# Recurrent outputs of three batches computed with tokens on the partitions, rows shifted by DMA, and loads and weight conversion placed earlier

## The chip, the cores and the metric

One core of a Trainium2 chip runs the whole kernel. The metric is the device time in microseconds (us) of that core, and the numbers compared are medians over runs. Profiles show one execution; its times count from the start of its span. Engines are called as in the profile: PE (TensorE, its weight loads PEld), DVE (VectorE), ACT (ScalarE), POOL (GpSimd), SP (the queue that issues every DMA here).

## What is computed

An mLSTM cell runs over 4 batches, 8 heads, 768 tokens and head size 40. Its output, laid side by side over the heads (320 features), goes through a Fourier mixing step and an MLP of width 1280. Everything is float32.

```python
for t in range(S):                                   # mLSTM, per batch and head
    m_new = max(f[t] + m, i[t])
    C = exp(f[t] + m - m_new) * C + exp(i[t] - m_new) * outer(v[t], k[t])
    n = exp(f[t] + m - m_new) * n + exp(i[t] - m_new) * k[t]
    y[t] = sigmoid(o[t]) * (C @ q[t]) / max(|n . q[t]|, 1)
...
u  = x + real(fft(fft(x, axis=1), axis=2))           # x: y, heads side by side
un = (u - mean(u)) / sqrt(var(u) + 1e-6)
out = u + relu(un @ w_ch1) @ w_ch2
```

## The kernel before

**Chunks and halves.** The recurrence is computed in 6 chunks of 128 tokens. In batch 0 a chunk is one block; in batches 1 to 3 (the second to the fourth; the code counts from 0) it is two halves of 64 tokens, so that TensorE works as four tiles of 64 rows by 64 columns and a product of one half and one head occupies one tile. For one such chunk (`plan_halves`, L726) the steps are: load q and k with features on partitions (`qk`), v and k with tokens on partitions (`kvt`), running maxima (`W<-M_d`), decays (`Gb<-G_d`) and the output gate (`so`); turn maxima into weights with 8 Exp on ACT (L464), mask them on POOL (L487), form the scores on PE (`halves_scores`, L603), multiply them into W on DVE (`halves_weigh`, L640); add this chunk's part to the state (`halves_to_state`, L614; decay on POOL L629, add on DVE L636/L638). The numerators and denominators come from two sets of products into PSUM tile `ph`: `halves_from_state` (L645, stationary a 40x64 block of the state, moving 64 scaled queries) and `halves_from_chunk` (L657, stationary 64x41 values, moving 64x64 weights W). It comes in two parts; between them ACT reads one element (`halves_between`, L668, shown as `warm`), so that the second part waits until the first has been written. All these products go through one helper line, L491, so rows of L491 are told apart by their tiles. A float32 product is two PE instructions.

**The turn.** `ph` then has features on partitions and tokens along the row. ACT copies it to SBUF (`mlstm_heads`, L559 to L579: one copy of 512, and for some chunks one or two copies of a single token; chunks named in `BACKWARDS` are copied in reverse), PE transposes it in four 128x128 steps (`halves_turn`, L677, shown at L681), and DVE divides, applies the gate and writes `x` (`mlstm_finish`, L684 to L703). The products and the transposes' result lie in one PSUM tile `heads` of two banks; `side(0)` and `side(1)` are its halves. The Fourier step pairs token t with token 768-t, hence the reversed chunks; token 0 of chunks 0, 1 and 2 changes place, by `h_first` and small copies.

**Order.** Nothing is scheduled by a tool: `at(slot, phase, fn)` writes work into a table, and it is emitted sorted by slot and phase (EVAC 0, FILL 1, MAIN 2, FILL_PE 3 within a slot), each engine and SP taking its own in that order. The MLP of one batch is spread over 32 slots (`MLP_SLOTS`) and the mLSTM of the next batch is laid between its products, 3 slots per chunk. Batch b's mLSTM begins in slot 0, 32, 50 and 82, its Fourier step in 22, 54, 83 and 115, its MLP in 31, 63, 95 and 127. Pairs of chunks are folded on DVE (`mix_fold`, L770) 18, 21 and 22 slots after the mLSTM began, the last one slot later in batches 2 and 3.

**Weights and early loads.** w_ch1 and w_ch2 arrive as ten pieces of float64 that are unpacked by integer work (`Piece`, L355): `take` is two DVE instructions, `convert` two on ACT, `join` three on DVE; the list `when` (L1308) gives each piece's slots, and from the sixth on a piece is loaded one slot after the join of the piece two before it. `gates` (L141) computes running maxima M and decays g for all batches, and `maxima_out` (L304) and `halves_of_chunks` (L307) write them to DRAM as M_d and G_d, from which each chunk loads.

The functions that the change touches, with what calls them:

Of the kernel before, what the change touches and what calls it, by code (L numbers as in the profile page):

```python
# [19 lines left out]
L = 128  # L20
# [20 lines left out]
BACKWARDS = (2, 4, 5)  # L41
PAIRS = ((0, 5), (1, 4), (2, 3))
ORDER = (0, 5, 1, 4, 2, 3)
M_INIT = -1.0e30
# [8 lines left out]
def kernel(  # L53
# [87 lines left out]
    def gates(gp):  # L141
# [44 lines left out]
        for t in hT_bufs + Cd_bufs:  # L186
            nc.gpsimd.memset(t, 0.0)
# [115 lines left out]

        def maxima_out():  # L304
            nc.sync.dma_start(out=M_d.rearrange("c i p t -> p c i t"), in_=M[0:BH].rearrange("p c (i t) -> p c i t", i=2))

        def halves_of_chunks(step):  # L307
# [8 lines left out]
            elif step == 1:  # L316
# [3 lines left out]
                nc.sync.dma_start(out=G_d[:, H:].rearrange("c p t -> p c t"), in_=g[H:BH])  # L320
# [12 lines left out]
            else:  # L333
                pt, pd = late["p2"]
                nc.vector.tensor_copy(out=colT[:, :, 1, H:], in_=pt[:, :, H:])
                nc.vector.tensor_copy(out=decB[:, NP:], in_=pd[:, NP:])

        at(12, FILL + 0.7, maxima_out)
        at(1, FILL + 0.2, parts, last)
# [9 lines left out]
        for n, (s, phase) in enumerate(((16, FILL + 0.2), (18, FILL + 0.3), (19, FILL + 0.4), (21, FILL_PE + 0.5),  # L349
                                        (26, FILL + 0.8))):  # L350
            at(s, phase, halves_of_chunks, n)
# [90 lines left out]
    def mlstm_queries(b, c):  # L442
        return slice(LH if b > 0 and c == 0 else 0, L)
# [40 lines left out]
    def mlstm_mask(b, c):  # L484
        for i in range(2):
            W = chunks[b, c].W[i * LH:(i + 1) * LH]
            nc.gpsimd.affine_select(out=W, in_=W, compare_op=OP.is_ge, fill=0.0, base=0, pattern=[[0, H], [1, LH]],  # L487
                                    channel_multiplier=-1)
# [70 lines left out]
    def mlstm_heads(b, c, ph, parts=False):  # L559

        k = chunks[b, c]
        hT, before = k.hT, hT_bufs[(b * NT + c - 1) % 2]
        if b > 0:
            hT, before = (t.rearrange("p (hip m) t -> p hip m t", hip=2) for t in (hT, before))
        every, first, later = (tuple([slice(None)] * (len(ph.shape) - 1) + [t]) for t in
                               (slice(0, L), slice(0, 1), slice(1, L)))
        if c in BACKWARDS:
            nc.scalar.copy(out=hT[later], in_=backwards(ph, L - 1, L - 1))
            if c > TG:
                nc.scalar.copy(out=hT[first], in_=ph[first])  # L570
            else:
                nc.gpsimd.tensor_copy(out=k.hT[:, :, 0:1], in_=h_first)
        else:
            for r in (slice(hip * 64, hip * 64 + D1) for hip in range(2)) if parts else (slice(0, L),):
                nc.scalar.copy(out=hT[r], in_=ph[r])
            if c == 0:
                nc.gpsimd.tensor_copy(out=h_first, in_=k.hT[:, :, 0:1])
        if 0 < c < TG:
            nc.scalar.copy(out=before[first], in_=ph[first])  # L579
# [14 lines left out]
    def side(n):  # L594
        return banks["heads"].rearrange("p hip (s m t) -> p s hip m t", s=2, t=L)[:, n]

    TILES = ((0, 0), (1, 1), (0, 1), (1, 0))

    def columns(c, n):

        return LH if c == 0 else n

    def halves_scores(b, c):  # L603
# [5 lines left out]
        for p in range(NP):  # L609
            for hip, i in TILES:  # L610
                r, t = slice(hip * 64, hip * 64 + D), slice(i * LH, (i + 1) * LH)
                product(k.ps[t, hip, p, :], k.qk[r, 1, p, t], k.qk[r, 0, p, t], True)

    def halves_to_state(b, c):  # L614
        k = chunks[b, c]
        for p in range(NP):
            for i, hip in TILES:
                if 2 * c + i < NS - 1:
                    r, h, n = slice(i * LH, (i + 1) * LH), hip * NP + p, columns(c, D)
                    product(k.pc[hip * 64:hip * 64 + n, i, p, :], k.k[r, h * D:h * D + n], k.vw[r, h, :], True)  # L620
# [11 lines left out]
    def halves_add(b, c, i):  # L632

        k, n = chunks[b, c], 2 * c + i
        if n == 0:
            nc.vector.tensor_copy(out=halves_state(k, 1), in_=k.pc[:, 0])  # L636
        elif n < NS - 1:
            nc.vector.tensor_tensor(out=halves_state(k, i + 1), in0=halves_state(k, i + 1), in1=k.pc[:, i], op=OP.add)  # L638
# [6 lines left out]
    def halves_from_state(b, c):  # L645

        k = chunks[b, c]
        k.ph = side(0)
        for m in range(2):
            for i in range(2):  # L650
                for hip, e in TILES:
                    if 2 * c + i > 0:
                        r, t, p = slice(hip * 64, hip * 64 + D), slice(i * LH, (i + 1) * LH), 2 * m + e
                        product(k.ph[e * 64:(e + 1) * 64, hip, m, t], k.C[i][r, p * D1:p * D1 + LH], k.qg[r, p, t],
                                m == 0 and i == (c == 0))

    def halves_from_chunk(b, c, turn):  # L657
# [4 lines left out]
        for m in range(2):  # L662
            for i, e in TILES:
                hip, n = i ^ turn, columns(c, D1)
                r, h = slice(i * LH, (i + 1) * LH), hip * NP + 2 * m + e
                product(k.ph[e * 64:e * 64 + n, hip, m, r], k.v[r, h * D1:h * D1 + n], k.W[r, h, :], False)

    def halves_between(b, c):  # L668

        nc.scalar.copy(out=warm[0:1, 0:1], in_=chunks[b, c].ph[0:1, 1, 1, L - 1:L])  # L670

    def halves_gather(b, c):
        k = chunks[b, c]
        k.hT = hT_bufs[(b * NT + c) % 2]
        mlstm_heads(b, c, k.ph)

    def halves_turn(b, c):  # L677
        k = chunks[b, c]
        px = side(0 if c == NT - 1 else 1)
        for p in range(NP):  # L680
            nc.tensor.transpose(px[:, p // 2, p % 2], k.hT[:, p, :], ident)  # L681
        k.px = px

    def mlstm_finish(b, c):  # L684

        k = chunks.pop((b, c))
        if c == 0:
            xs[b] = x_bufs[b % 2]
        px = k.px.rearrange("p (a pr) t -> p a pr t", a=2) if b == 0 else k.px
        h1 = px.rearrange("p a pr (two e) -> p a (pr two) e", two=2)  # L690
# [11 lines left out]
        x, sc = (t.rearrange("p (a h d) -> p a h d", a=2, d=D) for t in (xs[b][:, c, 0:DM], k.so))  # L702
        nc.vector.tensor_tensor(out=x, in0=h1[:, :, :, 0:D], in1=sc, op=OP.mult)  # L703

# [21 lines left out]
    def plan_halves(b, s0, stride=3):  # L726
        for c in range(NT):
            s = s0 + stride * c
            end = c == NT - 1
# [4 lines left out]
            at(s, FILL, mlstm_load_o, b, c)  # L734
# [10 lines left out]
            at(s + 1, MAIN + 0.7, halves_weigh, b, c)  # L745
            at(s + 3, MAIN - 0.1 if end else FILL_PE, halves_from_state, b, c)
            at(s + 3, MAIN - 0.1 if end else FILL_PE, halves_from_chunk, b, c, 0)
            at(s + 3, MAIN if end else FILL_PE + 0.5, halves_between, b, c)
            at(s + 3, FILL_PE + 3, halves_from_chunk, b, c, 1)
            at(s + 4, FILL - 0.6, halves_gather, b, c)  # L750
            at(s + 4, FILL + 0.35, mlstm_tanh, b, c)
            t = s0 + (7, 10, 13, 16, 19, 19)[c]
            at(t, FILL_PE + 0.5, halves_turn, b, c)
            at(t + 1, MAIN + 0.55, mlstm_finish, b, c)
# [519 lines left out]
    def plan_batch(b, s_mlstm, s_mix, s_mlp):  # L1274
# [9 lines left out]
        else:  # L1284
            feat = [s_mix + c for c in ((3, 4, 6) if b == 1 else (3, 4, 7))]
            add = [s_mix + c for c in ((4, 4, 5, 6, 7, 7) if b == 1 else (4, 4, 5, 6, 8, 9))]
# [13 lines left out]
    plan_batch(2, 50, 83, s_mlp + 2 * MLP_SLOTS)  # L1300
    plan_batch(3, 82, 115, s_mlp + 3 * MLP_SLOTS)
# [144 lines left out]
```

## Time and profile before

| | before |
|---|---|
| median of 5 runs | 405.69 us (403.64 to 408.04) |
| profiled execution: time, span | 405.69 us, 404.0 us |
| granted TensorE clock | 0.999 |
| PE busy | 388.4 us (96%) |
| DVE busy | 280.5 us (69%) |
| ACT busy | 181.7 us (45%) |
| POOL busy | 131.7 us (33%) |
| DMA | 43.29 MB, mean 107 GB/s |

Busy time counts an instruction from its start to its end; PE's instructions overlap, so what PE really spends on a group is read from the distance between the starts of successive rows of its timeline. A row of the timeline is: start in us, length in us, engine, line, operation, written tile, tiles read, shape of the stationary operand, shape of the moving one, count. In the list of groups a row's last part is the idle time of that engine just before the group, with the instruction that ended it. In the list of waits the three numbers are total us, times, longest us. In the table by stretch the columns are the stretch, its length, then busy us (and instructions) of PE, PEld, DVE, ACT and POOL, granted clock, DMA share and GB/s.

### The profile page before, as it was taken

How to read it: one execution, taken by the hardware profiler on the slowest of the kernel's cores; microseconds unless marked ns; L12 is line 12 of the kernel's file. 1: busy time of each engine (PE TensorE's matmuls, PEld its weight loads, DVE VectorE, ACT ScalarE, POOL GpSimd, SP SyncE). 2: the span in 40 equal slices, each digit the busy share in tenths (PEclk: the TensorE clock that was granted, in tenths of full speed). 3: DMA queues.
4: the chain of work that ended last, by engine and by line, in shares of the span. 5: the costliest groups of instructions: out<-in, count | busy, mean ns of one | idle time of the engine just before them, and what ended most of it. 6: DMA issues, size and time to landing. Idle time of an engine off the chain costs nothing.

```text
span 404.0 us, 10669 instructions
## 1 busy us (share of the span) xinstructions
PE 388.4 (96%) x4246; PEld 284.0 (70%) x4246; DVE 280.5 (69%) x669; ACT 181.7 (45%) x510; POOL 131.7 (33%) x228
## 2 busy tenths in 40 slices
PE   8999999989899999998999999989999999999996
PEld 6877555556567677755569898856469997556996
DVE  7799977699858448676864679966764785336652
ACT  6887258587561232653472334644440023455000
POOL 5646414388862442241162424431220000020000
PEclk9999999999999999999999999999999999999999
DMA  7889498488554154365010635200000000000000
GB/s 224 292 234 305 108 237 255 118 268 239 156 182 132 60 138 133 92 186 147 0 44 2 176 108 156 86 4 2 0 2 16 18 35 32 0 2 0 32 34 32
DMA packets 23836, 43.29 MB, mean 107 GB/s; under 512 B 5076, under 2 KB 12972, under 8 KB 23660
## 3 DMA queue, kind: packets, MB, share of 16 engines
q1 hardware_dynamic: 23788, 42.63, 36.0%
q8 instruction: 33, 0.54, 0.6%
q14 instruction: 15, 0.12, 0.1%
HBM read 38.49 MB, written 4.12 MB: 105 GB/s over the span
## 4 chain that ended last, share of the span: by engine, by line
PE 78%; DVE 9%; DMA 4%; ACT 3%; issue 3%; POOL 1%; SPq 1%; POOLq 0%; ACTq 0%; DVEq 0%
PE po L1203 17%; PE pm L1084 17%; PE po L1147 8%; PE pm L1089 5%; PE pm L1022 5%; PE ph L491 4%; PE ps L491 3%; DMA qk<-in_qkT 3%; PE pu L901 3%; PE ph L681 2%; PE pz L870 2%; DMA raw<-in_w 1%; PE pm L1013 1%; PE put L944 1%; PE pz L858 1%
## 5 line engine op out<-in xcount | busy, mean ns | idle before, releaser
L1153 DVE SCALAR_TENSOR_TENSOR x<-po,rstd,x 128x160 f32<-128x160 f32 (+1 forms) x69 | 26.9, 394 | 38.0 <-PE po L1203 35.3
L1093 DVE TENSOR_TENSOR h<-h,pm 128x384 f32<-128x384 f32 x60 | 30.7, 550 | 31.1 <-PE pm L1084 17.2
L1084 PE MATMUL pm<-uT,w_sb 128*128 128x384 f32 x90 | 37.3, 501 | 0.2 <-DVE uT L1072 0.2
L464 ACT ACTIVATE W<-W,colT 128x64 f32<-128x64 f32 x144 | 37.4, 341 | 0.0
L1147 PE MATMUL po<-w_sb,h 128*128 128x320 f32 x120 | 34.4, 435 | 0.0
L487 POOL TENSOR_SCALAR_AFFINE_SELECT W<-W 64x512 f32<-64x512 f32 x36 | 29.1, 808 | 15.5 <-ACT W L464 14.3
L629 POOL TENSOR_TENSOR C<-C,decB 128x164 f32<-128x164 f32 x30 | 17.2, 573 | 50.3 <-DVE C L638 44.9
L1022 PE MATMUL pm<-uT,w_sb 128*128 128x384 f32 x80 | 29.6, 499 | 0.1
L1147 PEld LDWEIGHTS po<-w_sb,h 128*128 128x128 f32 x120 | 22.2, 190 | 9.4 <-issue 0.6
L474 POOL TENSOR_TENSOR qg<-qk,Gb 128x512 f32<-128x512 f32 (+1 forms) x21 | 28.2, 1341 | 0.9 <-DMA Gb<-G_d 0.8
L1203 PE MATMUL po<-T,S 128*128 128x160 f32 x180 | 28.0, 302 | 0.3 <-DVE x L1153 0.3
L1203 PEld LDWEIGHTS po<-T,S 128*128 128x128 f32 x180 | 25.5, 190 | 1.8 <-DVE x L1153 0.5
L1203 PE MATMUL po<-w_sb,h 128*128 128x160 f32 x180 | 26.4, 301 | 0.0
L1203 PEld LDWEIGHTS po<-w_sb,h 128*128 128x128 f32 x180 | 25.1, 190 | 1.2 <-DVE x L1153 0.3
L1089 PE MATMUL pm<-uT,w1t_sb 64*128 64x384 f32 x120 | 25.4, 510 | 0.0
L968 POOL TENSOR_TENSOR t<-rstd 128x6 f32<-128x6 f32 x12 | 3.1, 256 | 65.3 <-DVE v L962 64.8
L1084 PEld LDWEIGHTS pm<-uT,w_sb 128*128 128x128 f32 x90 | 15.5, 189 | 12.5 <-DVE h L1093 3.6
L1140 ACT ACTIVATE h<-h 128x384 f32<-128x384 f32 x45 | 23.1, 520 | 2.0 <-DVE h L1093 2.0
L670 ACT COPY warm<-ph 1x1 f32<-1x1 f32 x18 | 2.6, 147 | 45.9 <-PE ph L491 41.8
L480 POOL TENSOR_TENSOR vw<-kvt,colT 128x328 f32<-128x328 f32 x23 | 18.7, 813 | 13.9 <-DMA kvt<-in_kv 10.8
L949 ACT COPY uT<-put 128x384 f32<-128x384 f32 x24 | 11.1, 476 | 26.1 <-PE put L944 26.1
L937 ACT ACTIVATE uc<-x 128x384 f32<-128x384 f32 x24 | 14.6, 617 | 14.8 <-DVE x L929 14.8
(233 smaller groups left out, 879.4 us busy)
## 6 DMA issues: line engine op xcount, KB each, us to landing
kvt<-in_kv SPq DMA_DIRECT2D x24, 336.0 KB
qk<-in_qkT SPq DMA_DIRECT2D x48, 160.0 KB
raw<-in_w SPq DMA_DIRECT2D x10, 640.0 KB
Gb<-G_d SPq DMA_DIRECT2D x36, 128.0 KB
W<-M_d SPq DMA_DIRECT2D x36, 128.0 KB
so<-in_o SPq DMA_DIRECT2D x24, 160.0 KB
out<-x SPq DMA_DIRECT2D x24, 160.0 KB
ds_sb<-in_dft_s SPq DMA_DIRECT2D x1, 1155.0 KB
```

The source lines that it names most:

```text
L464: nc.scalar.activation(out=k.W[:, h, :], in_=M, func=AF.Exp, scale=-1.0, bias=colT[:, c, 0, b * H + h:b * H + h + 1])
L474: nc.gpsimd.tensor_tensor(out=k.qg[:, :, t], in0=k.qk[:, 0, :, t], in1=k.Gb[:, :, t], op=OP.mult)
L487: nc.gpsimd.affine_select(out=W, in_=W, compare_op=OP.is_ge, fill=0.0, base=0, pattern=[[0, H], [1, LH]], channel_multiplier=-1)
L491: nc.tensor.matmul(out, w, x, start=start, stop=True, skip_group_check=True)
L1022: nc.tensor.matmul(k.pm[i], w1_sb[:, ch, f0:f0 + L], u[2 * ch], start=(ch == 0 and not ahead), stop=(ch == 1 and ahead), skip_group_check= ...
L1084: nc.tensor.matmul(bank, w, u, start=start, stop=True, skip_group_check=True)
L1089: nc.tensor.matmul(bank, block(w1t_sb, i)[rows], mlp_u(gr, 1)[rows], start=False, stop=True, skip_group_check=True)
L1093: nc.vector.tensor_tensor(out=h, in0=h, in1=bank, op=OP.add)
L1140: nc.scalar.activation(out=h, in_=h, func=AF.Relu, scale=-1.0)
L1147: nc.tensor.matmul(k.po, hidden(gr, f)[:, i * L:(i + 1) * L], w2_sb[:, f, :], start=(f == 0), stop=(f == NFF - 1))
L1153: nc.vector.scalar_tensor_tensor(out=u, in0=po, scalar=k.rstd[:, c:c + 1], in1=u, op0=OP.mult, op1=OP.add)
L1203: nc.tensor.matmul(po, a[:, f], w[:, f], start=start and f == 0, stop=f == half - 1, skip_group_check=True)
```

## The change

In batches 1 to 3 the operands of the output products change places: the scaled queries and W become stationary (64 columns each) and the state and the values move (41 columns each), so `ph` has tokens on partitions. `halves_gather` and `halves_turn` go; `mlstm_finish` reads `ph` itself, one slot after the products. In chunks 0, 1 and 3 (the new `BACKWARDS`, for all batches) queries are laid out in reverse by the host, so their rows come out reversed; as a shift by one row is left over, their finish writes into `so` and `halves_rows` moves the rows into `x` by DMA, with two small POOL copies for chunk 2. For odd head pairs the two halves of keys and values are exchanged (in the host's layout, and on chip by `other_halves` and by an exchanged index in `maxima_out`), and the state's add reads PSUM with one more dimension. M and g are reversed for the backward chunks on POOL before they are written out. In the plan: batch 2 begins in slot 53 and batch 3 in 83; the output gate is loaded a slot sooner; tanh and finish come sooner; five pieces of w_ch2 are unpacked up to three slots sooner; one `mix_add` comes a slot later.

```diff
-BACKWARDS = (2, 4, 5)
+BACKWARDS = (0, 1, 3)
+RUNS = ((0, 2, True), (2, 3, False), (3, 4, True), (4, 6, False))
...
+        def other_halves():
+            odd = [colT[i * LH:(i + 1) * LH, :, 0, H + 1:BH:2] for i in range(2)]
+            kept = gp.tile([LH, NT, (BH - H) // 2], FP, name="kept")
+            for out, in_ in ((kept, odd[0]), (odd[0], odd[1]), (odd[1], kept)):
+                nc.gpsimd.tensor_copy(out=out, in_=in_)
         def maxima_out():
-            nc.sync.dma_start(out=M_d.rearrange("c i p t -> p c i t"), in_=M[0:BH].rearrange("p c (i t) -> p c i t", i=2))
+            m, in_ = (t.rearrange("p (n t) -> p n t", t=LH) for t in (free[0:BH, 0:S], flat(M, slice(0, NT))))
+            for c0, c1, back in RUNS:
+                n = slice(2 * c0, 2 * c1)
+                nc.gpsimd.tensor_copy(out=m[:, n], in_=backwards(in_[:, n], LH - 1, LH) if back else in_[:, n])
+            m = m.rearrange("p (c i) t -> p c i t", i=2)
+            for odd in range(2):
+                for i in range(2):
+                    nc.sync.dma_start(out=M_d[:, i ^ odd, odd:BH:2].rearrange("c p t -> p c t"), in_=m[odd:BH:2, :, i])
...
-                nc.sync.dma_start(out=G_d[:, H:].rearrange("c p t -> p c t"), in_=g[H:BH])
+                for c0, c1, back in RUNS:
+                    v = g[0:BH, c0:c1]
+                    if back:
+                        v = turned[:, at_:at_ + c1 - c0]
+                        at_ += c1 - c0
+                        nc.gpsimd.tensor_copy(out=v, in_=backwards(g[0:BH, c0:c1], L - 1, L))
+                    nc.sync.dma_start(out=G_d[c0:c1, H:].rearrange("c p t -> p c t"), in_=v[H:BH])
...
-                nc.vector.tensor_copy(out=colT[:, :, 1, H:], in_=pt[:, :, H:])
+                nc.vector.tensor_copy(out=colT[:, :, 1, H:BH:2], in_=pt[:, :, H:BH:2])
+                for i in range(2):
+                    nc.vector.tensor_copy(out=colT[i * LH:(i + 1) * LH, :, 1, H + 1:BH:2],
+                                          in_=pt[(1 - i) * LH:(2 - i) * LH, :, H + 1:BH:2])
...
+        at(13, FILL + 0.7, other_halves)
...
     def halves_from_state(b, c):
-        k.ph = side(0)
-        ...
-                        product(k.ph[e * 64:(e + 1) * 64, hip, m, t], k.C[i][r, p * D1:p * D1 + LH], k.qg[r, p, t], ...)
+        k.ph = banks["heads"][:, :, 0:NP * D1].rearrange("p hip (m d) -> p hip m d", d=D1)
+        ...
+                    product(k.ph[t, hip, p, :], k.qg[r, p, t], k.C[i][r, p * D1:(p + 1) * D1], p == 0)
     def halves_from_chunk(b, c, turn):
-                product(k.ph[e * 64:e * 64 + n, hip, m, r], k.v[r, h * D1:h * D1 + n], k.W[r, h, :], False)
+                product(k.ph[queries(c, i), hip, p, :], k.W[rows(j), h, :], k.v[rows(j), h * D1:(h + 1) * D1],
+                        2 * c + i == 0 and m == turn == 0)
-    def halves_gather(b, c):
-        ...
-    def halves_turn(b, c):
-        ...
     def mlstm_finish(b, c):
-        px = k.px.rearrange("p (a pr) t -> p a pr t", a=2) if b == 0 else k.px
-        h1 = px.rearrange("p a pr (two e) -> p a (pr two) e", two=2)
+        h1 = k.px.rearrange("p (a pr) (two e) -> p a (pr two) e", a=2, two=2) if b == 0 else k.ph
...
+        k.x = k.so if b > 0 and c in BACKWARDS else xs[b][:, c, 0:DM]
...
+    def halves_rows(b, c):
+        x, y = xs[b][:, :, 0:DM], chunks[b, c].x
+        def move(out, in_):
+            nc.sync.dma_start(out=out, in_=in_)
+        if c == 2:
+            nc.gpsimd.tensor_copy(out=x[0:1, 1], in_=x[0:1, 2])
+            nc.gpsimd.tensor_copy(out=x[0:1, 2], in_=x[0:1, 0])
+            move(x[0:1, 0], chunks[b, 1].x[L - 1:L])
+        elif c in BACKWARDS:
+            move(x[1:L, c], y[0:L - 1])
+            if c != 1:
+                move(x[0:1, c], y[L - 1:L])
...
-            at(s, FILL, mlstm_load_o, b, c)
+            at(s - 1, FILL, mlstm_load_o, b, c)
...
-            at(s + 1, MAIN + 0.7, halves_weigh, b, c)
-            at(s + 3, MAIN - 0.1 if end else FILL_PE, halves_from_state, b, c)
-            at(s + 3, MAIN - 0.1 if end else FILL_PE, halves_from_chunk, b, c, 0)
-            at(s + 3, MAIN if end else FILL_PE + 0.5, halves_between, b, c)
+            at(s + 1, FILL + 0.55 if b == 1 and c > 0 else MAIN + 0.7, halves_weigh, b, c)
+            at(s + 3, FILL_PE, halves_from_state, b, c)
+            at(s + 3, FILL_PE, halves_from_chunk, b, c, 0)
+            at(s + 3, FILL_PE + 0.5, halves_between, b, c)
             at(s + 3, FILL_PE + 3, halves_from_chunk, b, c, 1)
-            at(s + 4, FILL - 0.6, halves_gather, b, c)
-            at(s + 4, FILL + 0.35, mlstm_tanh, b, c)
-            t = s0 + (7, 10, 13, 16, 19, 19)[c]
-            at(t, FILL_PE + 0.5, halves_turn, b, c)
-            at(t + 1, MAIN + 0.55, mlstm_finish, b, c)
+            at(s + 3, FILL_PE + 0.6, mlstm_tanh, b, c)
+            at(s + (5 if (b, c) == (2, 2) else 4), FILL + 0.3 if b == 1 else MAIN + 0.55, mlstm_finish, b, c)
+            at(s + 6, FILL - 0.6, halves_rows, b, c)
...
-            add = [s_mix + c for c in ((4, 4, 5, 6, 7, 7) if b == 1 else (4, 4, 5, 6, 8, 9))]
+            add = [s_mix + c for c in ((4, 4, 5, 6, 7, 7) if b == 1 else (4, 5, 5, 6, 8, 9))]
...
-    plan_batch(2, 50, 83, s_mlp + 2 * MLP_SLOTS)
-    plan_batch(3, 82, 115, s_mlp + 3 * MLP_SLOTS)
+    plan_batch(2, 53, 83, s_mlp + 2 * MLP_SLOTS)
+    plan_batch(3, 83, 115, s_mlp + 3 * MLP_SLOTS)
...
-    when += [((33, 0.7), (35, 0.7), (36, 0.6))] + [((s, 0.7), (s + 1, 0.7), (s + 2, 0.6)) for s in (36, 39, 42, 45)]
+    when += [((33, 0.7), (34, 0.3), (34, 0.6)), ((34, 0.7), (35, 0.7), (36, 0.6))]
+    when += [((s, 0.7), (s + 1, 0.7), (s + 2, 0.6)) for s in (36, 39, 42)]
```

## The prediction, made before the change was run

> **What bounds the kernel now.** I read the page first: shares of the engines, then the chain that ended last, then the list of waits, then timelines and stretches.
>
> ```profile
> PE 388.4 (96%) x4246; PEld 284.0 (70%) x4246; DVE 280.5 (69%) x669; ACT 181.7 (45%) x510; POOL 131.7 (33%) x228
> ...
> PE 78%; DVE 9%; DMA 4%; ACT 3%; issue 3%; POOL 1%; SPq 1%; POOLq 0%; ACTq 0%; DVEq 0%
> ...
> L681 PE MATMUL ph<-ident,h 128*128 128x128 f32 x72 | 10.6, 276 | 0.0
> ```
>
> PE is busy nearly all the time and is 78% of the chain, so PE work that disappears should shorten the run, except in stretches where PE is only kept waiting. The 10.6 us of the turn are overlapping durations; what it really holds PE for is the distance between starts:
>
> ```profile
> 180.86 0.60 PE L681 MATMUL ph<-ident,h 128*128 128x128 f32 x4
> 181.30 0.81 PE L1084 MATMUL pm<-uT,w_sb 128*128 128x384 f32 x2
> ```
>
> Four transposes of a chunk cost 181.30 - 180.86 = 0.44 us. Next, where PE waits, and for whom:
>
> ```profile
> PE ph L491 <- DVE x L703: 3.9, 5, 1.3
> ...
> PE ph L491 <- ACT warm L670: 0.7, 1, 0.7
> PE ph L491 <- DVE W L643: 0.5, 1, 0.5
> ```
>
> The first is five waits of `halves_from_state` for the finish of an earlier chunk. The other two lie in one stretch that is not PE's:
>
> ```profile
> 75.00:105.00 30.00, 27.54 (x468) 16.43 (x469) 29.21 (x57) 22.18 (x63) 25.01 (x34) 1.00 0.77 218
> ```
>
> There DVE is busy 29.2 of 30 us and POOL 25.0: the mLSTM of batch 1 beside the unpacking of w_ch2. What PE saves there is not simply time saved.
>
> [...]
>
> ```profile
> 139.97 0.69 PE L491 MATMUL ph<-qg,C 40*64 40x64 f32 x32
> 140.49 0.41 PE L491 MATMUL ph<-W,kvt 64*41 64x64 f32 x16
> 140.71 0.65 PE L491 MATMUL ps<-qk 40*64 40x64 f32 x32
> 141.18 0.49 PE L491 MATMUL ps<-vw,kvt 64*40 64x41 f32 x32
> 141.49 0.41 PE L491 MATMUL ph<-W,kvt 64*41 64x64 f32 x16
> ...
> 116.22 0.63 PE L491 MATMUL ps<-vw,kvt 64*64 64x41 f32 x32
> 116.66 0.41 PE L491 MATMUL ph<-W,kvt 64*41 64x64 f32 x16
> ```
>
> By starts, 32 instructions cost 0.47 us with 64 stationary and 64 moving columns (140.71 to 141.18), 0.31 with 40 and 41 (141.18 to 141.49), but 0.44 with 64 and 41 (116.22 to 116.66). The last is the form of all new output products. So fewer moving columns bring next to nothing: the 64 stationary columns are the limit[...].
>
> **The change part by part.**
>
> *Turn.* 18 chunks x 0.44 = 7.9 us of PE go. Four of the 18 (86 to 111 us: L681 starts at 86.4, 94.8, 101.9, 110.6) lie in or next to the stretch where DVE and POOL set the pace; I count those 1.8 us as nothing. Gain 6.1, at most 7.9.
>
> *Output products.* From state 0.52 to about 0.47 to 0.50, from chunk 0.22 + 0.34 (the second to its successor at 141.83) to about the same plus 0.02, as the stationary side grows from 41 to 64 columns. I take 0; bounds from -1 us (gain) to +0.7 over 18 chunks.
>
> *Waits for the finish.* Now the finish of chunk c - 1 is planned in slot s + 1 and the next products into `ph` in slot s + 3, where s begins chunk c; before, the finish of chunk 3 stood in slot s0 + 17 and chunk 5's products in s0 + 18. Chunk 5's products of batches 2 and 3, 32 slots apart, started at 183.4 and 272.7 us in the timeline, so a slot is about 2.8 us, and the five DVE instructions of a finish are 0.16 + 0.17 + 0.20 + 0.64 + 0.49 = 1.66 us. Of 3.9 us I count 3.5.
>
> *ACT.* The copies of 18 chunks go (18 x 0.58 and a dozen of 0.17 to 0.18: about 12.6 us), but ACT is busy 45%; on the path they count only through L670, whose element read must run between two groups of products. For chunk 5 nothing of another kind now stands between the two groups, so PE waits there for the products' end, ACT's 0.15 us and two hand-overs: in the trace a chunk 5 showed 0.58 us of PEld waiting for it even with other products between. I charge 0.2 us x 3 = 0.6; bounds 0 to 1.5. Tanh (0.48) comes ahead of nothing PE needs.
>
> *DVE.* Finish is the same five instructions with another source. The state's add keeps its 164 elements (0.32). Weigh of batch 1 comes forward in its slot, ahead of the unpacking's long instructions. A piece is 0.64 + 0.68 + 0.95 + 1.25 + 1.09 = 4.6 us of DVE, 0.83 + 0.73 on ACT, and one 0.36 us issue on SP; five pieces move up to 3 slots ahead. From 65 to 75 us DVE was busy only 4.6 of 10 us, and can take one. The stretch held PE for 30 - 27.5 = 2.5 us; with a piece's DVE work out of it I count 1.0 regained, bounds -1 to 2.5. A join that waits for ACT now holds the adds behind it on DVE for at most ACT's 1.6 us.
>
> *POOL.* Chunk 2 gets two copies of 1x320. The nearest row, a copy of 1x161, took 0.66 us, so about 1.0 each; 2 us per batch, less the old `h_first` copies (0.41 each). For batches 2 and 3 POOL has room (7.3 us busy of 160 to 180). In batch 1 it doesn't: qg of chunk 4 ended at 106.8, its products started at 107.9. The copies sit ahead of that qg, so up to 1.5 us of PE wait; I charge 0.5. Before that they wait for DVE's finish and a landed row; masks and decays queue behind them.
>
> *Rows by DMA.* 6 issues per batch, 18 x about 0.35 us of SP. Row moves are issued at s + 6, the folds read them 3 slots later at least (chunk 3: s0 + 15, fold s0 + 18): 8 us of cover. [...] No run here shows such a move, nor SP's own price for it. Cost 0[...]. Loads behind them have 5 slots.
>
> *Early part.* M_d takes four issues instead of one and waits for four POOL copies, about 2 us (from a 32x384 row of 1.09 us); behind it on SP are the Fourier tables, issued at 32.5 and first used at 44.4. G_d takes four, behind two POOL copies: SP waited 8.3 us there for ACT until 44.7, now about 1.8 us more; behind it are batch 1's first loads, and SP next waited 1.5 us at 50.4 for a raw buffer, which absorbs most. `other_halves` is about 1 us of POOL. I charge 0.5; bounds 0 to 2.5, as the chain runs through a 6.6 us load at 54.8. The gate loaded a slot sooner (0.4 us of SP) needs one of four buffers that the row move must first release; it has a slot. The later starts of batches 2 and 3 (3 and 1 slots) leave their folds 7 and 9 slots ahead of the Fourier products; the `mix_add` a slot later stays ahead of its turn. Cost 0.
>
> **Sum:** 6.1 + 0 + 3.5 + 1.0 - 0.6 - 0.5 - 0.5 = 9.0 us. The profiled execution took 405.69 us (span 404.0), equal to the median: 405.7 - 9.0 = 396.7; I say 396.5.
>
> **Rivals.**
>
> *The columns count after all.* If 41 moving columns cost as 40/41 did (0.31 per 32), each chunk would save (0.52 + 0.56) - 0.62 = 0.46, times 18 = 8 us more: 388.5. Against it stands the 0.44 measured; even half of it gives 392. Chance 0.12.
>
> *New waits take the gain.* In 63 to 113 us DVE and POOL set the pace, and a faster PE merely waits; if the same holds in 225 to 260 us (DVE 28.4 of 35 us), another 1.5 us of turns and half of the 3.5 go, and the three costs reach their upper ends (5.5 for 1.6): 396.7 + 1.5 + 1.8 + 3.9, about 404. For it: 29.2 of 30. Against: from 120 us on PE shows almost no wait but those that go. Chance 0.17.
>
> *Row moves arrive late, slower than before.* SP takes its work in order and was held up to 5.9 us by a W load waiting for PE. A move stuck behind one comes 8 us later than planned, and a fold then stops DVE, with weigh and the MLP's adds behind it. It decides once a move lands more than 3 slots late: with 6 us in each of three batches, 18 us, against 9 gained, 415. Against it: the moves are emitted before the loads of their slot, and the page's W waits end with the slot. Chance 0.05.
>
> *The change doesn't do what it says:* products as before, no turn but the same stalls: 405.7 - 6.1 + 1.6, about 401. It is in the range.
>
> **Chances.** My forecast 0.66, columns 0.12, new waits 0.17, late rows 0.05. About 1% (4 us: 401.6 to 409.7) is what a measurement of this kernel can tell from no change. Faster by more: 0.66 + 0.12 + a quarter of the new waits = 0.82; within: 0.13; slower: 0.05. The range is 389 to 402: it takes in my bounds and most of the columns case.
>
> **What would show it.** No L681, PE's busy time down by 8 us or more; no wait for L703; blocks of 32 output products still 0.44 to 0.5 us apart; DVE busier at 65 to 75 us. Wrong would be: output products at 0.31, PE waiting for qg or W in 80 to 113 us by more than before, DVE's folds waiting for DMA, or the first MLP products later than before.

## The result, and the profile after

| | before | after |
|---|---|---|
| median | 407.11 us (403.57 to 410.51, 80 runs) | 408.72 us (406.85 to 411.00, 43 runs) |
| ratio to before, 95% interval | | 1.0049, 1.0033 to 1.0065 |
| profiled execution: time, span | 405.69, 404.0 us | 410.13, 408.4 us |

Half a per cent slower, where 396.5 us was forecast. The turn is gone, and yet nothing is gained. The page of the kernel after (busy time, the granted clock in 40 slices, the shares of the chain that ended last):

```profile
PE 385.9 (94%) x4174; PEld 280.4 (69%) x4174; DVE 278.7 (68%) x671; ACT 171.8 (42%) x481; POOL 133.0 (33%) x237
...
PEclk9999999899969999999999999999999999999999
...
PE 60%; DVE 22%; DMA 9%; issue 3%; ACT 2%; SPq 1%; POOL 1%; DVEq 0%; ACTq 0%; POOLq 0%
```

PE fell from 78% to 60% of the chain, DVE rose from 9% to 22%, DMA from 4% to 9%, and there are dips in the clock. PE's busy time fell by only 2.5 us, though transposes of 10.6 us went: a matmul on a slower clock is busy longer (those of L1053 start 0.64 us apart at half clock and 0.32 at full, below; with the row moves split, below, it is 380.5 us, 7.9 less than before). In PE's list of waits, the finish (now L720) is down from 3.9 to 0.4 us, as forecast; other rows take its place:

```profile
PE ph L519 <- ACT warm L699: 6.9, 8, 2.4
PE po L1234 <- DVE x L1184: 2.5, 3, 1.1
PE pm L1115 <- DVE h L1124: 1.3, 2, 1.0
...
PE ps L519 <- POOL vw L507: 1.2, 1, 1.2
...
PE ps L519 <- DMA qk<-in_qkT: 0.7, 2, 0.4
...
PE ph L519 <- DVE x L720: 0.4, 1, 0.4
```

**Where it is lost.** The first transpose of each batch's MLP (tile `put`) is an easy landmark. The stages between these landmarks, in us, from the starts of those rows in the timelines (this kernel and the experiments below). Each row is from one profiled execution. The two rows that begin batch 1's MLP, before and then after:

```profile
156.66 0.55 PE L944 MATMUL put<-ident,uc 128*128 128x128 f32 x3
```

```profile
163.53 0.55 PE L975 MATMUL put<-ident,uc 128*128 128x128 f32 x3
```

| kernel | to batch 0's `put` | to batch 1's | to batch 2's | to batch 3's | to the end |
|---|---|---|---|---|---|
| before | 56.0 | 100.7 | 83.4 | 84.3 | 79.6 |
| after | 55.8 | **107.7** | 83.6 | 80.5 | 80.8 |
| row moves of 112 + 15 | 54.7 | 99.7 | 83.6 | 80.5 | 80.9 |
| row moves of 126 + 1 | 55.2 | 99.4 | 83.5 | 80.5 | 80.9 |
| row moves of 113 + 14 | 55.8 | 101.9 | 83.6 | 80.5 | 81.0 |
| 112 + 15 in batch 1 alone | 54.9 | 99.6 | 83.7 | 80.5 | 81.1 |
| before, with nine moves of 127 | 55.4 | **104.3** | 83.4 | 84.3 | 79.7 |
| before, with nine of 112 + 15 | 55.8 | 99.4 | 83.4 | 84.7 | 79.8 |

The fourth stage gains 3.8 us of the 4.5 that its five turns (5 x 0.44 = 2.2) and its share of the finish's waits (2.3) promised. The third, with six turns, gains nothing; by its later start batch 2 has a chunk more to do there. The second, with batch 1's mLSTM in it, loses 7.0. Stretches of it (columns as in the table of stretches before), after, and then before:

```profile
60.00:130.00 70.00, 61.68 (x891) 36.59 (x890) 49.28 (x100) 35.79 (x106) 35.89 (x54) 0.93 0.62 171
...
111.00:117.00 6.00, 1.94 (x64) 1.50 (x64) 0.33 (x1) 3.44 (x13) 3.78 (x8) 0.92 0.25 72
117.00:123.00 6.00, 6.00 (x14) 3.19 (x10) 2.12 (x6) 0.59 (x2) 1.67 (x6) 0.52 0.70 171
```

```profile
60.00:130.00 70.00, 67.27 (x1112) 41.85 (x1112) 56.43 (x116) 42.29 (x127) 43.06 (x60) 1.00 0.67 195
```

In the 70 us, every engine and the DMA do less than before: no engine's share has risen, everybody waits. Between 111 and 117 us PE works 1.94 of 6 us and DVE 0.33; in the next 6 us PE is busy throughout, but on a clock of 0.52. In the trace PE runs at half clock from 116.0 to 122.8 us, 6.8 us, and the matmuls of L1053 start 0.64 us apart there instead of 0.32, which is 2.9 us on top of the wait. In the 3.4 us ahead (the length of the shorter of such stretches) PE worked 0.36 us, and its wait at 116 us was 2.4 us. In this case's profiles twelve more such stretches began between 70 and 240 us, each 3.4 or 6.8 us long; one is in this kernel, from 78.4 to 81.9 us, begun 1.7 us after a wait of 1.5 us for `warm` had ended. In the 3.4 us ahead of the twelve PE was busy for 1.4 to 2.2 us, and no wait there was longer than 2.7 us. So in these profiles waits of 1.2 to 2.7 us were followed by 3.4 or 6.8 us at half clock; what sets it off isn't shown. None of the changed kernel's executions had a mean clock above 0.995; of the 43 executions of the kernel before that ran beside the first experiments, 26 had 0.999 or more.

What they wait for stands in the chain of the kernel after (start, length, what):

```profile
98.27 2.92 SPq L454
...
101.66 11.09 DMA kvt<-in_kv
112.76 0.02 issue
112.77 0.03 SPq L728
...
112.83 0.65 SPq L728
113.48 0.05 issue
113.53 10.53 DMA x<-so
...
124.16 0.50 DVE eo L809
```

L728 is the issue of a row move, x<-so. The pair of moves issued around 113 us takes until 124, when DVE's fold can start; the load of keys and values issued 4 us after an earlier one takes 11.1. On SP's queue the same moves hold up the issues behind them (first the kernel after, then the one with rows split into 112 and 15):

```profile
97.55 0.68 SPq L728 DMA_DIRECT2D x<-so  x1
98.27 3.35 SPq L454 DMA_DIRECT2D qk<-in_qkT  x2
101.66 0.35 SPq L456 DMA_DIRECT2D kvt<-in_kv  x1
...
118.16 6.31 SPq L478 DMA_DIRECT2D Gb<-G_d  x2
```

```profile
111.57 1.28 SPq L478 DMA_DIRECT2D Gb<-G_d  x2
```

The 6.31 us are not spent in issuing. The two issues of `Gb` take 0.62 and 0.59 us in the trace, and between them SP waits 5.1 us for a row move to land. The loads don't need the moved rows, nor does L728 need the keys and values that it stands behind in the chain. In the trace SP's issues use eight completion semaphores (counters that tell that a transfer has landed) in turn: 240 issues, each semaphore 30 times, always eight issues apart, and an issue waits on the semaphore it uses, so until the transfer eight issues before it has landed. So a slow move also stops SP itself, eight issues later. SP's waits for row moves between 60 and 130 us, 16.6 us in all and none with the rows split:

```profile
SPq L478 <- DMA x<-so: 11.2, 2, 6.1
...
SPq L484 <- DMA x<-so: 5.4, 1, 5.4
```

**Theory A.** The 127 rows are the cause, by their number. In the trace this kernel's last move of 127 rows goes row by row, 127 packets mostly 52 ns apart and 55 ns each, and takes 6.8% of the 16 DMA engines, about one engine's share (the window is shown below). That the row count decides this was the author's assumption, not yet shown by a trace: 112 or 126 rows would be spread over several engines, and 113, a prime as 127 is, again over one. The experiments measure these counts. A move on one engine is slow itself, and by this theory every later load on 16 engines has a sixteenth of its rows on that engine, behind it. The packets of the load of keys and values issued at 101.66 us (128 packets of 2688 bytes, counted from the trace by start) look so:

| us | 102 to 103 | 103 to 104 | 104 to 105 | 105 to 106 | 106 to 111 | 111 to 113 |
|---|---|---|---|---|---|---|
| packets | 5 | 52 | 57 | 6 | 0 | 8 |

Eight is 128/16, one engine's share, though the trace doesn't name a packet's engine. The load is 120 rows done by 106 us, and the last eight come when a row move has passed. **Rival theories:** the new loads and moves are simply more DMA work; the earlier unpacking of weights crowds DVE; the finish and the element reads in their new slots make PE wait.

### The profile page after: what moved, and what is told of

Same layout as the page of the kernel before. It is cut to its first block, busy times and chain, and to the rows that moved or that the text cites. A ratio compares the mean times of both kernels' runs of the same rounds, so it can differ in the third digit from the quotient of the medians.

```text
span 408.4 us, 10572 instructions
## 1 busy us (share of the span) xinstructions
PE 385.9 (94%) x4174; PEld 280.4 (69%) x4174; DVE 278.7 (68%) x671; ACT 171.8 (42%) x481; POOL 133.0 (33%) x237
## 4 chain that ended last, share of the span: by engine, by line
PE 60%; DVE 22%; DMA 9%; issue 3%; ACT 2%; SPq 1%; POOL 1%; DVEq 0%; ACTq 0%; POOLq 0%
PE po L1234 17%; PE pm L1115 13%; PE po L1178 8%; DMA x<-so 5%; PE pm L1120 4%; DMA kvt<-in_kv 3%; PE pu L932 3%; PE ph L519 2%; PE ps L519 2%; DVE m L422 2%; DMA raw<-in_w 2%; DVE so L716 1%; DVE e L420 1%; PE pz L901 1%; PE pz L889 1%
## 5 line engine op out<-in xcount | busy, mean ns | idle before, releaser
L491 ACT ACTIVATE W<-W,colT 128x64 f32<-128x64 f32 x144 | 37.4, 338 | 9.7 <-DMA W<-M_d 9.7
L652 POOL TENSOR_TENSOR C<-C,decB 128x164 f32<-128x164 f32 x30 | 16.0, 534 | 75.4 <-DVE C L667 63.6
L1115 PE MATMUL pm<-uT,w_sb 128*128 128x384 f32 x90 | 37.6, 505 | 2.0 <-DVE h L1124 1.3
L1053 PE MATMUL pm<-uT,w_sb 128*128 128x384 f32 x80 | 32.9, 554 | 0.1
L515 POOL TENSOR_SCALAR_AFFINE_SELECT W<-W 64x512 f32<-64x512 f32 x36 | 27.3, 759 | 11.2 <-ACT W L491 9.6
L999 POOL TENSOR_TENSOR t<-rstd 128x6 f32<-128x6 f32 x12 | 3.3, 274 | 80.3 <-DVE v L993 79.7
L1115 PEld LDWEIGHTS pm<-uT,w_sb 128*128 128x128 f32 x90 | 15.6, 189 | 16.5 <-DVE h L1124 7.4
L1053 PEld LDWEIGHTS pm<-uT,w_sb 128*128 128x128 f32 x80 | 16.2, 216 | 11.8 <-issue 5.0
L1120 PE MATMUL pm<-uT,w1t_sb 64*128 64x384 f32 x120 | 23.4, 508 | 0.0
L519 PE MATMUL ph<-kvt,W 64*64 64x41 f32 x576 | 16.2, 231 | 7.0 <-ACT warm L699 6.9
```

The lines of the kernel that those rows point to most:

```text
L491: nc.scalar.activation(out=k.W[:, h, :], in_=M, func=AF.Exp, scale=-1.0, bias=colT[:, c, 0, b * H + h:b * H + h + 1])
L519: nc.tensor.matmul(out, w, x, start=start, stop=True, skip_group_check=True)
L1053: nc.tensor.matmul(k.pm[i], w1_sb[:, ch, f0:f0 + L], u[2 * ch], start=(ch == 0 and not ahead), stop=(ch == 1 and ahead), skip_group_check= ...
L1115: nc.tensor.matmul(bank, w, u, start=start, stop=True, skip_group_check=True)
L1120: nc.tensor.matmul(bank, block(w1t_sb, i)[rows], mlp_u(gr, 1)[rows], start=False, stop=True, skip_group_check=True)
```

## The experiments

Each ran beside the kernel before; ratios are to it, with 95% intervals, and a time is the median of that experiment's executions.

**Rows in two pieces, 112 and 15.**

```diff
-            move(x[1:L, c], y[0:L - 1])
+            move(x[1:113, c], y[0:112])
+            move(x[113:L, c], y[112:L - 1])
```

> Only edit to the changed kernel: each row move of 127 rows is issued as two, of 112 and of 15 rows. Theory A (a move of 127 rows runs on one DMA engine, holds it for about 10 us and delays every later load's share on that engine): the moves land within 3 us, the kernel takes about 397 us, ratio to before 0.97 to 0.985. Rival B (the new order of ACT and DVE work in batch 1, with the products' second part waiting for the element read, costs the time by itself): within 2 us of the changed kernel, ratio 1.00 to 1.01.

Measured: 401.10 us, ratio 0.9855 (0.9814 to 0.9897). The same bytes, with nine more issues on SP, and 7.6 us less than the changed kernel (7.9 by the two ratios). That is just outside theory A's 0.970 to 0.985 and far from rival B's 1.00. This one beats both kernels, and none of the later versions can be told from it as faster.

**No row moves.** Left out: rows of the reversed chunks 0, 1 and 3 stay one token off; their finish writes straight into `x`.

```diff
-        k.x = k.so if b > 0 and c in BACKWARDS else xs[b][:, c, 0:DM]
+        k.x = xs[b][:, c, 0:DM]
...
-            move(x[0:1, 0], chunks[b, 1].x[L - 1:L])
-        elif c in BACKWARDS:
-            move(x[1:L, c], y[0:L - 1])
-            if c != 1:
-                move(x[0:1, c], y[L - 1:L])
```

> The changed kernel without any row move by DMA: the rows of the reversed chunks stay unshifted, so this part of the computation is left out. It bounds what the moves cost in all. Theory A: no more than 2 us faster than the split moves, about 396 us, ratio 0.965 to 0.985. Rival B: as the changed kernel, 1.00 to 1.01.

Measured: 404.69 us, 0.9936 (0.9908 to 0.9965): neither theory's outcome, and the run tells less than it was meant to. Its profiled execution took 401.29 us at a clock of 1.000. Only three of the 22 executions had that clock (401.0 to 401.7 us); the other 19, at 0.982 to 0.996, took 403.6 to 409.1, and none of them has a profile, so what slowed them isn't shown. In the profile, the finish now writes `x` two slots sooner than the moves did, into a buffer that is still being stored: its L720 waited 2.0 us for a store, and PE behind it 2.4 us at 245.7 us, so the fourth stage is 82.4 us instead of 80.5. The second is the shortest of all, 97.5 us against 99.7 with split moves, whose profile has 3.4 us of half clock there; whether split moves still cost anything, this run can't tell.

**The moves alone, in the kernel before**, as nine transfers of 127 rows of 1 KB into a spare tile that nobody reads; then the same in 112 and 15 rows.

```diff
+    def spare_rows(b, c):
+        nc.sync.dma_start(out=rest[1:L], in_=done[b, c].so[0:L - 1, 0:2 * L])
...
+            if c in (0, 1, 3):
+                at(t + 3, FILL - 0.6, spare_rows, b, c)
```

> The kernel before, with nine moves of 127 rows of 1 KB (from the gate tile to an unused one) added two slots after the finish of chunks 0, 1 and 3 of batches 1 to 3. Theory A: slower than before by 3 to 9 us, ratio 1.007 to 1.022, with loads behind the moves landing up to 10 us late. Rival B: no change, 0.998 to 1.003.

> The kernel before with the same nine added moves as in the earlier run with 127 rows, cut into 112 and 15 rows. Theory A: the added bytes and issues cost nothing that shows, ratio to before 0.998 to 1.004. If the bytes, the SP issues or the wait for the gate tile were the cost, 1.006 to 1.010 as with 127 rows.

Measured: 410.29 us, 1.0081 (1.0056 to 1.0105), and 405.59 us, 0.9982 (0.9958 to 1.0005). So transfers with no reader cost some 3.6 us (410.29 against 406.64 beside them), and nothing measurable when cut in two. The stage table puts all of it into the second stage. Between 60 and 130 us SP waited 12.9 us for these moves of 127, and not at all for the cut ones.

**Other cuts: 113 and 14, then 126 and 1.** They separate the row count itself from the number or length of the pieces.

```diff
-            move(x[1:L, c], y[0:L - 1])
+            move(x[1:114, c], y[0:113])
+            move(x[114:L, c], y[113:L - 1])
```

```diff
-            move(x[1:L, c], y[0:L - 1])
+            move(x[1:L - 1, c], y[0:L - 2])
+            move(x[L - 1:L, c], y[L - 2:L - 1])
```

> As the split into 112 and 15 rows, with the same number of DMAs, but cut into 113 and 14 rows; 113 is a prime like 127. [...] the first move again runs on one engine for about 9 us and the kernel takes 406 to 409 us, nearly as changed. If two smaller DMAs are what helps, it takes 401 us like the 112 and 15 split.

> As the changed kernel, with each move of 127 rows issued as 126 rows and 1 row. Theory A [...]: as the split into 112 and 15, about 401 us (400 to 403), each move landed 2 to 3 us after its issue. Rival: the size of the longest piece decides, so 126 rows in one piece behave like 127 (408) or like 113 (406), above 405.

Measured: 405.98 us, 0.9977 (0.9957 to 0.9998), and 401.11 us, 0.9843 (0.9798 to 0.9888). One row less than 127 in the long piece recovers everything; fourteen less, a prime number of rows again, recover only part of it. The last row move of each kernel has the DMA queues almost to itself. The DMA part of the profile in just those windows (packets; then the hardware queue's packets, MB and share of 16 engines), for 127 rows, 7.5 us long, and for 126 and 1, 1.0 us long:

```profile
DMA packets 161, 0.18 MB, mean 24 GB/s; under 512 B 33, under 2 KB 160, under 8 KB 160
...
q1 hardware_dynamic: 160, 0.16, 6.8%
```

```profile
DMA packets 170, 0.16 MB, mean 163 GB/s; under 512 B 44, under 2 KB 170, under 8 KB 170
...
q1 hardware_dynamic: 170, 0.16, 54.5%
```

6.8% is one engine of sixteen (6.25%) and a few small packets. By their starts, the 127 packets ran from 274.13 to 281.51 us, mostly 52 ns apart, each taking 55 ns: one after another. For 126 and 1 they ran from 265.36 to 266.20 us, several at a time. With 113 and 14 they ran from 268.39 to 275.06 us, as slowly row by row as the 127, and SP waited 14.6 us for moves between 60 and 130 us, nearly as in the changed kernel. That it nevertheless gave back 2.7 us of the 7.6 is more than its 11% fewer rows. A part may be the clock: the median over its executions is 0.992, and 0.987 in the changed kernel, which by an estimate is up to 2.0 us (0.005 of 408). Why it dips less there is left open.

**Split in batch 1 alone.**

```diff
+            n = 112 if b == 1 else L - 1
-            move(x[1:L, c], y[0:L - 1])
+            move(x[1:n + 1, c], y[0:n])
+            if n < L - 1:
+                move(x[n + 1:L, c], y[n:L - 1])
```

> The changed kernel, its 127-row moves split into 112 and 15 rows in batch 1 alone; batches 2 and 3 keep 127 rows. If only the dense loads of batch 1 make the one-engine moves cost time, the time is that of the split everywhere, 401 to 402 us, and the stretches after the first MLP turn of batch 1 are as with the split. Rival: every move costs about the same (7.6 us over nine): two thirds of the loss stay, 406 us.

Measured: 402.62 us, 0.9885 (0.9841 to 0.9928). The rival's 406 is out; the interval overlaps the full split's. SP still waits for the slow moves of batches 2 and 3 in this run:

```profile
SPq L478 <- DMA x<-so: 10.1, 3, 5.0
...
SPq L484 <- DMA x<-so: 2.4, 1, 2.4
```

12.5 us of waiting on SP cost no more than 0.3 us there by the stage table (the last three stages together). Those loads seem to have slots to spare (DMA share 0.36 from 180 to 280 us with the split, against 0.67 from 60 to 130). In batch 1 such waits stop the kernel.

**Weights unpacked as before** (on top of 112 + 15).

```diff
-    when += [((33, 0.7), (34, 0.3), (34, 0.6)), ((34, 0.7), (35, 0.7), (36, 0.6))]
-    when += [((s, 0.7), (s + 1, 0.7), (s + 2, 0.6)) for s in (36, 39, 42)]
+    when += [((33, 0.7), (35, 0.7), (36, 0.6))] + [((s, 0.7), (s + 1, 0.7), (s + 2, 0.6)) for s in (36, 39, 42, 45)]
```

> The split moves of 112 and 15 rows, and the pieces of w_ch2 unpacked in the slots of the kernel before. If unpacking sooner helps as forecast (1 us), this is 0 to 2 us slower than the split moves alone. If the sooner unpacking is what delays the element read on ACT (theory B in part), it is faster than them by 2 us or more.

Measured: 402.98 us, 0.9891 (0.9846 to 0.9936), overlapping the split alone. The sooner unpacking is neither the loss nor clearly a gain.

**Element reads ahead of ACT's conversions** (on top of 112 + 15). With the split, PE's largest wait is still `warm`, 3.7 us. In batch 1 ACT's read of one element stands behind a `convert` that waits for DVE.

```diff
-    when += [((33, 0.7), (34, 0.3), (34, 0.6)), ((34, 0.7), (35, 0.7), (36, 0.6))]
-    when += [((s, 0.7), (s + 1, 0.7), (s + 2, 0.6)) for s in (36, 39, 42)]
+    when += [((33, 0.7), (34, 0.3), (34, 0.6)), ((34, 0.7), (35, 2.55), (36, 0.6))]
+    when += [((s, 0.7), (s + 2, 2.55), (s + 3, 0.6)) for s in (36, 39, 42)]
```

> The split into 112 and 15 rows, with the two ACT instructions of each of four w_ch2 pieces put behind the element read of the same stretch (joins one slot later in three of them). Theory: the reads of batch 1 are late because they stand behind a convert that waits for DVE's take; the waits of 1.1 and 1.3 us at 75 and 85 us go, and with them about 2 us: 399 to 400 us. Rival: DVE sets the pace from 75 to 90 us, so PE waits as long elsewhere: no difference to the split alone, 401 to 402.

Measured: 402.06 us, 0.9870 (0.9824 to 0.9916). The reads' waits at 75 and 85 us went, and DVE's took their place (1.86 us for the state's add L667 at 83.5 us), which is the rival's outcome.

**Chunk 5's products as before**, without and with the previous edit.

```diff
-            at(s + 3, FILL_PE, halves_from_state, b, c)
+            end = c == NT - 1
+            at(s + 3, MAIN - 0.1 if end else FILL_PE, halves_from_state, b, c)
```

(and likewise the first part of `halves_from_chunk` and `halves_between`)

> Split moves of 112 and 15 rows, and chunk 5's first products and element read back in their phases of the kernel before, with MLP products between the two groups. Three waits of PE for the element read (0.43 us each at the ends of the three batches) go: 0.5 to 1.3 us faster than the split run. If the earlier phase makes these products wait for the finish of chunk 4 instead, 0 to 2 us slower.

> As the run with the converts behind the reads, and chunk 5's products and element read back in the slots of the kernel before. If the two waits are separate costs, 0.5 to 1 us below that run; if that part is worth nothing, as it was beside the split alone, the same within 0.5.

Measured: 401.63 us, 0.9880 (0.9839 to 0.9922), and 401.98 us, 0.9862 (0.9810 to 0.9913). No difference can be measured, though in the first the split kernel's three waits of 0.43 us for the read, at 116, 189 and 274 us, did go; PE's wait for the finish (L720) rose from 0.4 to 1.0 us instead.

**The `mix_add` slot as before**, in batches 2 and 3, then in batch 3 alone.

```diff
-            add = [s_mix + c for c in ((4, 4, 5, 6, 7, 7) if b == 1 else (4, 5, 5, 6, 8, 9))]
+            add = [s_mix + c for c in ((4, 4, 5, 6, 7, 7) if b == 1 else (4, 4, 5, 6, 8, 9))]
```

> Split moves of 112 and 15 rows, and the mix_add of chunk 5 back in its slot of the kernel before. If two mix_adds in one slot are what makes PE wait for DVE's residual add in batches 2 and 3 (1.2 us each, at 233 and 320 us of the split run), 1.0 to 2.4 us faster than the split run, 399 to 400 us, without those two waits. If DVE is just as late otherwise, no change from 401 us.

> As the split into 112 and 15 rows, with the mix_add back in its old slot in the last batch alone (batch 2 keeps the later slot). In the profiles, the stretch from the last batch's MLP turn to the end is 79.6 us before and 80.9 with the later slot. If the later slot costs that in the last batch and serves batch 2, the last stretch returns to about 79.7 and the others stay: 400 us, 1.2 below the split alone. Rival: batch 3 needs the later slot as batch 2 does (88.1 for 83.6 us there), and the fourth stretch grows by 2 us or more: 402 to 405.

Measured: 403.39 us, 0.9919 (0.9893 to 0.9944), and 400.77 us, 0.9850 (0.9802 to 0.9899). So the old slot in both batches is 2.3 us slower than the split alone, against both outcomes that were named. By stages, the third is 88.1 us with the old slot in batch 2 against 83.6, and the last 79.7 against 80.9 with it in batch 3. In the third, PE's wait for the residual add (L1185) is longer and half clock follows it; of 4.5 us the wait is 1.6 and the half clock 2.7 (the same 20 matmuls in 5.63 us instead of 2.91). The row of the wait with the old slot (split alone: 1.08):

```profile
234.54 3.04 PE L1235 MATMUL po<-T,S 128*128 128x160 f32 x10 [2.72 <-DVE x L1185]
```

This profile has the lowest clock of that kernel's 14 executions (0.986; eight have 0.996), so 4.5 us is more than most of them lose. Batch 2 is better off with the later slot, and the last batch pays 1.2 us for it; of these the fourth stage takes back 0.5, and the gain from giving it up there is within the noise of the medians.

**Batches 2 and 3 starting in slots 50 and 82.**

```diff
-    plan_batch(2, 53, 83, s_mlp + 2 * MLP_SLOTS)
-    plan_batch(3, 83, 115, s_mlp + 3 * MLP_SLOTS)
+    plan_batch(2, 50, 83, s_mlp + 2 * MLP_SLOTS)
+    plan_batch(3, 82, 115, s_mlp + 3 * MLP_SLOTS)
```

> The split into 112 and 15 rows, with batch 2 beginning in slot 50 and batch 3 in slot 82 as in the kernel before. Theory: the new PE waits for DVE at 233, 245, 259, 265 and 320 us (together about 4 us beyond the kernel before) come from DVE work of batches 2 and 3 laid onto the Fourier steps by the later starts; with the old starts they fall, and the time is 398 to 400 us. Rival: they follow from the finish standing earlier beside other DVE work, or the reclaimed PE time runs into a DVE that is the limit there anyway: 400.5 to 402.5, with the waits elsewhere.

Measured: 404.31 us, 0.9935 (0.9904 to 0.9966): slower than the split alone, outside what either theory gave. Stages: 102.6, 81.3, 82.5, 81.0 against 99.7, 83.6, 80.5, 80.9. A chunk goes back from the third to the second stage, and the fourth loses 2.0, so by this profile the later start of batch 3 is worth about that. Of the second stage's 2.9 us some is chance: at 67 us, before any edited slot, DVE waited 4.34 us for a weight load here and 2.17 in the split kernel, and PE then had 6.8 us of half clock for 3.4. The three of 19 executions with a clock of 0.999 or more took 400.6 to 401.6 us, as the split kernel's three did (400.6 to 401.3), so much of the difference between the medians comes with half clock.

## Why the prediction was wrong

**The step that failed: *Rows by DMA*, "Cost 0".** It gave the moves 8 us of cover. From issue to landing they took 9.2 us with the queues almost empty (7.4 from the first packet to the last) and 11.0 to 13.0 in batch 1, where one delayed a fold on DVE (L809) by 4.6 us: no cover was left. Most of the price was at another place, which the sum put at nothing with "Loads behind them have 5 slots": a slow move delays the loads issued after it, and those had no slots to spare in batch 1. They are late in two ways, the share of a load's rows that comes only when the move has passed, and SP's wait for the transfer eight issues before; no run separates the two. The 7.6 us between 408.72 and 401.10 are the cost; the stage table puts 8.0 of the 9.1 us between the two profiled spans into one stage. There, PE's waits by the lists are 3.9 us longer (`warm` 6.9 for 3.7, `vw` 1.2, `qk` 0.7, less 1.2 for the state's add), and the half clock from 116 us adds 2.9; 1.2 us isn't assigned.

**The rival *Row moves arrive late*** had the right object, the right sign and the wrong mechanism: no move was stuck behind a W load. W loads were stuck behind moves (ACT's L491 waited 9.3 us for W until 113.6), and it cost time in one batch, not three, so its 415 was too high. Its chance of 0.05 was too low for an operation that no trace had shown.

**Turn and finish: right.** L681 is gone, and the finish's waits fell from 3.9 to 0.4 as counted (3.5). The fourth stage gained 3.8 us with five turns (2.2) and its part of those waits (2.3).

**Output products: right.** The 64 stationary columns set the pace. Timeline of the kernel after:

```profile
101.38 0.68 PE L519 MATMUL ph<-C,qg 40*64 40x41 f32 x32
101.87 0.42 PE L519 MATMUL ph<-kvt,W 64*64 64x41 f32 x16
102.10 0.67 PE L519 MATMUL ps<-qk 40*64 40x64 f32 x32
```

32 instructions (16 products of two each) cost 0.49 us (101.38 to 101.87) with 41 moving columns; the state products were 0.52 with 64. The rival that columns count falls.

**New waits: undersized.** With the moves repaired the gain is 5.5 us, not 9.0. Against the kernel before, the split kernel's profile shows the turn's 7.9 and the finish's 3.5 us gone, and in exchange PE waits for `warm` (+3.0), for the residual add L1185 (+2.2), for the MLP's add L1125 (+1.3), for the state's add L667 (+1.2) and for L1104 (+0.4), which prepares the MLP's operands, less 0.7 for rows that went: 7.4 us, and 1.3 more at half clock at 87 us. That leaves 2.7; the span from the first `put` on fell by 3.4, so 0.7 isn't assigned. The prediction had charged 0.6 net for such waits (0.6 + 0.5 + 0.5 - 1.0). In its term *ACT* the read at the end of each batch costs 0.3 us for the 0.2 charged; two reads in batch 1, of 1.1 and 1.4 us behind a `convert`, weren't foreseen. Another of these waits, in the split kernel, PE and then DVE:

```profile
233.12 1.08 PE L1235 MATMUL po<-T,S 128*128 128x160 f32 x6 [1.08 <-DVE x L1185]
```

```profile
230.92 0.49 DVE L716 SCALAR_TENSOR_TENSOR so<-so,den 128x320 f32<-128x320 f32 x1
231.45 0.49 DVE L720 TENSOR_TENSOR so<-ph,so 128x320 f32<-128x320 f32 x1
231.86 0.68 DVE L672 TENSOR_TENSOR W<-ps,W 128x512 f32<-128x512 f32 x1
232.45 0.31 DVE L667 TENSOR_TENSOR C<-C,ps 128x164 f32<-128x164 f32 x1
232.69 0.67 DVE L1185 SCALAR_TENSOR_TENSOR x<-po,rstd,x 128x160 f32<-128x160 f32 x2
```

The finish, in its sooner slot, is directly ahead of weigh, add and the L1185 that PE waits for. The rival *New waits take the gain* (404) was right that a faster PE would wait for DVE in these stretches; with the moves repaired its 404 was too high. Three edits that took such waits away (reads ahead, chunk 5, the `mix_add`) moved them and left the time, which speaks for a shortage of DVE time there rather than for one wrong slot; it wasn't shown further.

**Smaller terms.** The two row copies on POOL took 0.44 and 0.45 us, not 1.0 each. The early part's 0.5 can't be told from chance: the first `put` came between 54.7 and 56.6 us in kernels that do the same work up to there. The sooner unpacking's 1.0 isn't seen. The later `mix_add`, "cost 0", cost 1.2 us in the last stage and bought up to 4.5 in the third.

## What to carry to other kernels

Before a DMA is planned, factor its row count: a shift by one turns 128 rows into 127, a prime, whose packets took 7.4 us one after another (113, also prime, 6.7 us; 126 and 1 together 0.8), and one extra issue (126 + 1, or 112 + 15) bought back 7.6 us. Other counts weren't measured as such moves. A slow transfer's cost is looked for in the loads issued behind it and in the queue that issues them, above all where every engine becomes less busy at once, not only at its own reader. An operation that the trace doesn't show deserves a rival with a real chance, and a cost range that reaches to its worst form.

## What the runs showed of the hardware, unexpected

- Six of the nine one-engine moves cost at most 0.3 us, though SP waited 12.5 us for them; the three in batch 1 cost 8.0. A transfer's price lay mostly in what was queued behind it.
- PE's clock fell to half for 3.4 or 6.8 us after waits of 1.2 to 2.7 us, with PE busy for up to 2.2 of the 3.4 us before. With the old `mix_add` slot, 1.6 us more of waiting was followed by a loss of 2.7 us at half clock.
- An issue directly behind a move of 127 rows took longer: for a single row 1.40 to 3.31 us in five of six cases of the changed kernel, and 0.54 to 0.57 behind split moves. What holds SP inside an issue isn't shown. Rows that merge two `Gb` issues look the same (6.31 and 7.03 us), but those hold SP's waits of 5.1 and 6.1 us for a landing.
- DVE's unpacking instructions L422 and L426 on 128x640 take 0.82 us each with POOL idle, and 1.1 to 1.9 us in eight of the twelve cases with POOL at work during them (split kernel, ten of each). That is up to 2.3 times; what in POOL's work lengthens them isn't shown. It is part of why batch 1's stretch has so little DVE time to spare.
